# Fewer and wider score visits, a GLU in chunks of 256 tokens with gate and up in one bank, and attention output turned by DMA

## The chip, the cores and the metric

One core of a Trainium2 chip runs the whole program. The metric is the device time of one execution in microseconds. Three runs of the kernel before took 642.13 to 642.98 us, median 642.45.

## The reference

Two layers, each an attention part A and a gated part B, each with a residual, on x of 2048 tokens by 512 (bfloat16). Both layers use the same weights.

```python
def A(x, wqkv, wo):                      # 32 heads of 16, window of 256
    q, k, v = heads(x @ wqkv)
    s = q @ k.T * 16 ** -0.5
    s = where(0 <= i - j < 256, s, -1e9)
    return merge(softmax(s) @ v) @ wo
def B(x, w_gate, w_up, w_down):          # 512 -> 1792 -> 512
    return (sigmoid(x @ w_gate) * (x @ w_up)) @ w_down
for layer in range(2):
    x = x + A(layernorm(x), wqkv, wo)
    x = x + B(layernorm(x), w_gate, w_up, w_down)
```

## The kernel before, in words

Tokens stand in 16 tiles of 128. Scores are computed transposed: keys of tile t on the partitions, queries of tiles t, t+1 and t+2 (the window of 256) along the columns. A **visit** fills one PSUM tile, Sps (four banks, one buffer, line 335), by matmuls that use a quarter of the array's rows each (four heads side by side, `tile_position`), and one exp on ScalarE (line 339) writes the result to a ring in SBUF, PTring, of six slots per head. A visit before covers four heads and three query tiles, 1536 columns; at tiles 14 and 15 there are two or one query tile and 1024 or 512 columns. Eight visits make a key tile, 128 a layer, 256 in all. The ring's slots for the three query tiles are not always neighbours, so a visit takes one, two or three runs of four matmuls (`pieces`).

VectorE multiplies the diagonal block by a triangle (line 346), GpSimd clears the far corner of the third block (`affine_select`, line 351). When the three key tiles that a query tile needs are there, `values` (line 364) makes 48 small matmuls for half of the heads into OTps; VectorE copies that out as OTs (line 369). One visit later TensorE turns OTs by four transposes into PSUM (tps, line 381), VectorE divides by the row sums (Rt, line 389; On, line 391), SyncE issues a DMA transpose (OnT, line 395), and two visits later `oproj` (line 417) multiplies by wo; VectorE adds the residual (line 419) and begins the layer norm (lines 152 to 162), whose output a DMA transpose turns into xnT (line 174).

The projections take four tiles (512 tokens) at a time: q and k in chunks of 128 columns (line 237), v per tile (line 254), copied out by ScalarE. The GLU takes chunks of 128 of the 1792 columns: four gate matmuls (line 283) into one PSUM buffer, a tanh on ScalarE (line 286), four up matmuls (line 293) into another, and on VectorE hT = (tanh + 1) x up (line 295); w_down is halved once, so that this is the sigmoid. Then 14 down matmuls a tile (line 305). It does 512 tokens at a time, except that four of its ten streams take 256.

The order is made by a planner in `run`. It goes through the visits; in each it first issues the scores and the exp, then values where they are due, then what has been put off to this visit (`at`), and then pops units from the first stream that is ready (projections and GLU, in the order of a list) until the estimated TensorE time of the visit, T_SLOT, is used up. Each engine runs its instructions in that order. All of proj_ps, v_ps, gps, ups, dps, tps and OPps share three PSUM buffers (`ps_d`). The planner's figures only set the order; they are no times of the chip.

Of the kernel before, what the change touches and what calls it, by code (L numbers as in the profile page):

```python
# [8 lines left out]
ALU = mybir.AluOpType  # L9
# [33 lines left out]


class Stream:
# [5 lines left out]
    def add(self, ns, tag, fn):  # L51
        self.units.append((ns, tag, fn))

    def pop(self, done):
        ns, tag, fn = self.units.pop(0)
        fn()
        done.add(tag)
        return ns


class Net:
# [3 lines left out]
    def __init__(self, ctx, tc, A_x, wqkv, wo, w_gate, w_up, w_down, out):  # L65
# [17 lines left out]
        self.ontp = pool("on_t", 4)  # L83
# [14 lines left out]
        self.hT = big.tile([P, FC, TGW], BF16, name="hT")  # L98
# [32 lines left out]
        self.left = {}  # L131
        self.states = {}
# [68 lines left out]
    def proj_stream(self, kinds, L, tg):  # L201
        key = ("p", L, tg)
        gi = L * NTG + tg
        free = 0
        if "k" in kinds and gi >= 2:
            free = TGW // P * SLOTS_T * (gi - 1)
        if "v" in kinds and gi >= 3:
            free = max(free, (4 * (gi - 3) + 6) * SLOTS_T + 10)
        s = Stream(key, free)
        s.needs = [(key, t) for t in range(tg * NBG, (tg + 1) * NBG)]  # L210
        self.left[key] = self.left.get(key, 0)
# [19 lines left out]
    def _qk(self, key, tg, b, k, cq):  # L231
# [3 lines left out]
        c0 = (k == "k") * D + cq * P  # L235
        for kt in range(KT):
            nc.tensor.matmul(pt[:], lhsT=self.wq[:, kt, c0:c0 + P], rhs=xnT[:, kt, :],  # L237
                             start=(kt == 0), stop=(kt == KT - 1))
        self.used_up(key)
        if k == "q":  # L240
            nc.scalar.copy(out=self.qT[:, cq, tg * TGW:(tg + 1) * TGW], in_=pt[:])
            return
        kt = self.ktp.tile([P, TGW], BF16, name="kt")
        nc.scalar.copy(out=kt[:], in_=pt[:])
        for e in range(2):
            nc.vector.tensor_scalar(out=self.kTp[b][:, cq, e, :], in0=kt[:],
                                    scalar1=self.rms[e][:, 0:1], scalar2=None, op0=ALU.mult)

    def _v(self, key, tg, b, tt):
# [7 lines left out]
        nc.scalar.copy(out=vdst, in_=pt[:].rearrange("p (h e) -> p h e", e=16))  # L257
        self.used_up(key)

    def glu_stream(self, L, t0, n):  # L260
# [8 lines left out]
        for fc in range(FC):  # L269
            s.add(KT * (w / 2.4 + 3), None, lambda fc=fc: self._gate(key, fc, c0, w))  # L270
            s.add(KT * (w / 2.4 + 3), None, lambda fc=fc: self._up(key, fc, c0, w, last))
        cuts = [0, 5, 10, FC]
        for tt in range(n):
            for a, b in zip(cuts, cuts[1:]):
                s.add((b - a) * T_MM, ("d", L, t0 + tt, b), lambda tt=tt, a=a, b=b: self._down(L, t0 + tt, tt, a, b))
        return s

    def _gate(self, key, fc, c0, w):
# [6 lines left out]
        self.th = self.sigp.tile([P, TGW], BF16, name="gth")  # L285
        nc.scalar.activation(out=self.th[:, 0:w], in_=ps[:, 0:w], func=AF.Tanh, scale=0.5)  # L286

    def _up(self, key, fc, c0, w, last):
# [3 lines left out]
        for kt in range(KT):  # L292
            nc.tensor.matmul(ps[:, 0:w], lhsT=self.wu[:, kt, fc * P:(fc + 1) * P], rhs=xnT[:, kt, c0:c0 + w], start=(kt == 0),  # L293
                             stop=(kt == KT - 1))
        nc.vector.scalar_tensor_tensor(out=self.hT[:, fc, 0:w], in0=self.th[:, 0:w], scalar=1.0, in1=ps[:, 0:w],  # L295
                                       op0=ALU.add, op1=ALU.mult)
        if fc == FC - 1 and last:
            del self.xnT[key]

    def _down(self, L, t, tt, a, b):  # L300
# [6 lines left out]
        if b == FC:  # L307
            nc.vector.tensor_tensor(out=self.xsb[:, t, :], in0=self.xsb[:, t, :], in1=self.dps[:], op=ALU.add)
# [4 lines left out]

    def scores(self, L, t, g):
        nc = self.nc
        cq, e = g // 2, g % 2
        N = min(3 * P, S - t * P)
        nb = N // P  # L320
        order = sorted(range(nb), key=lambda b: ring_slot(t, b))
        p0 = ring_slot(t, order[0])
        step = ring_slot(t, order[1]) - p0 if nb > 1 else 1
        pieces = []
        for i, b in enumerate(order):
            if pieces and pieces[-1][1] + pieces[-1][2] == b:
                pieces[-1][2] += 1
            else:
                pieces.append([i, b, 1])
        kTp = self.kTp[(L * NTG + t // NBG) % 2]  # L330
        ko = (t % NBG) * P
        sps = self.sps
        for i, b, n in pieces:
            for m in range(4):
                nc.tensor.matmul(sps[:, m, i * P:(i + n) * P], lhsT=kTp[32 * m:32 * m + 32, cq, e, ko:ko + P],  # L335
                                 rhs=self.qT[32 * m:32 * m + 32, cq, (t + b) * P:(t + b + n) * P],
                                 start=True, stop=True, tile_position=(32 * m, 0))
# [239 lines left out]
```

## Time and profile before

| | |
|---|---|
| profiled execution | 641.7 us, its span 640.0 us |
| median of three runs | 642.45 us |
| first exp starts | 14.8 us |
| last exp starts | 583.8 us |
| busiest engines | TensorE 580.9 us, ScalarE 460.4 us, VectorE 423.5 us |
| exps | 256, 352.2 us of ScalarE |
| score matmuls | 1984 |
| transposes of OTs on TensorE | 256 matmuls, 25.6 us by modelled ends |

The span is the time from the first to the last instruction of the program on its engines. Rows of a timeline read: start, time taken, engine, line, operation, output and inputs, shape, count of merged instructions, and in brackets the engine's idle time ahead of it and what ended it. A group's row ends with its busy time, the mean time in ns of one, and the engine's idle time ahead of them. PE is TensorE, PEld its weight loads, ACT ScalarE, DVE VectorE, POOL GpSimd, SP SyncE.

### The profile page before, as it was taken

How to read it: one execution, taken by the hardware profiler on the slowest of the kernel's cores; microseconds unless marked ns; L12 is line 12 of the kernel's file. 1: busy time of each engine (PE TensorE's matmuls, PEld its weight loads, DVE VectorE, ACT ScalarE, POOL GpSimd, SP SyncE). 2: the span in 40 equal slices, each digit the busy share in tenths (PEclk: the TensorE clock that was granted, in tenths of full speed). 3: DMA queues.
4: the chain of work that ended last, by engine and by line, in shares of the span. 5: the costliest groups of instructions: out<-in, count | busy, mean ns of one | idle time of the engine just before them, and what ended most of it. 6: DMA issues, size and time to landing. Idle time of an engine off the chain costs nothing.

```text
span 640.0 us, 16976 instructions
## 1 busy us (share of the span) xinstructions
PE 580.9 (91%) x7216; PEld 281.8 (44%) x7216; DVE 423.5 (66%) x851; ACT 460.4 (72%) x497; POOL 166.4 (26%) x191
## 2 busy tenths in 40 slices
PE   4886789897779999899989999989999999999997
PEld 2333454553234444444434444444444444444675
DVE  5875577766556658865588666975766676665533
ACT  3998677787868897766877897679877886762221
POOL 3443223313323223310143222432222333100000
PEclk9998799999879999999999999999999999999999
DMA  7664400111100001100011000210011001101100
GB/s 229 106 169 116 127 18 19 23 26 27 18 13 18 17 18 24 34 18 17 19 34 34 16 17 18 43 27 14 11 27 42 18 18 34 31 18 27 38 18 16
DMA packets 63771, 24.95 MB, mean 39 GB/s; under 512 B 51664, under 2 KB 63696, under 8 KB 63696
## 3 DMA queue, kind: packets, MB, share of 16 engines
q1 hardware_dynamic: 63696, 23.87, 15.9%
q8 instruction: 56, 0.92, 0.6%
q14 instruction: 19, 0.16, 0.1%
HBM read 9.70 MB, written 2.10 MB: 18 GB/s over the span
## 4 chain that ended last, share of the span: by engine, by line
PE 58%; ACT 16%; DVE 14%; issue 6%; DMA 4%; POOL 1%; ACTq 0%; POOLq 0%; DVEq 0%
PE ups L293 13%; PE gps L283 13%; ACT PTring L339 13%; PE dps L305 9%; PE Sps L335 7%; PE OTps L364 5%; PE OPps L417 4%; DMA OnT<-On 3%; DVE ln_stats L152 3%; DVE xn L162 3%; DVE PTring L346 2%; PE proj_ps L237 2%; PE v_ps L254 2%; PE tps L381 2%; DVE OTs L369 1%
## 5 line engine op out<-in xcount | busy, mean ns | idle before, releaser
L339 ACT ACTIVATE PTring<-Sps 128x1536 bf16<-128x1536 f32 (+2 forms) x256 | 352.2, 1376 | 76.4 <-PE Sps L335 68.3
L351 POOL TENSOR_SCALAR_AFFINE_SELECT PTring<-PTring 128x1024 bf16<-128x1024 bf16 x112 | 127.3, 1138 | 168.3 <-ACT PTring L339 166.8
L295 DVE SCALAR_TENSOR_TENSOR hT<-gth,ups 128x512 bf16<-128x512 bf16 (+1 forms) x140 | 81.1, 579 | 74.7 <-PE ups L293 63.8
L283 PE MATMUL gps<-xnT,wg 128*128 128x512 bf16 (+1 forms) x560 | 122.7, 342 | 4.5 <-DMA xnT<-xn 2.1
L293 PE MATMUL ups<-xnT,wu 128*128 128x512 bf16 (+1 forms) x560 | 121.6, 340 | 3.4 <-DVE hT L295 2.3
L286 ACT ACTIVATE gth<-gps 128x512 bf16<-128x512 f32 (+1 forms) x140 | 71.5, 512 | 73.8 <-PE gps L283 71.4
L335 PE MATMUL Sps<-qT,kTp 32*128 32x128 bf16 (+2 forms) x1984 | 86.9, 246 | 27.5 <-ACT PTring L339 24.5
L305 PE MATMUL dps<-wd,hT 128*128 128x512 bf16 x448 | 108.3, 380 | 0.0
L155 POOL TENSOR_TENSOR ln_rs<-ln_rs,nhalf 128x1 f32<-128x1 f32 x64 | 38.3, 598 | 263.9 <-DVE ln_rs L154 259.1
L346 DVE TENSOR_TENSOR PTring<-PTring,maskq 128x1024 bf16<-128x1024 bf16 x128 | 97.2, 760 | 2.4 <-ACT PTring L339 2.4
L335 PEld LDWEIGHTS <-kTp 32*128 32x128 bf16 x1984 | 39.7, 92 | 129.1 <-issue 124.1
L283 PEld LDWEIGHTS <-wg 128*128 128x128 bf16 x560 | 51.4, 99 | 44.3 <-issue 7.6
L293 PEld LDWEIGHTS <-wu 128*128 128x128 bf16 x560 | 51.2, 98 | 41.9 <-issue 8.8
L237 PE MATMUL proj_ps<-xnT,wq 128*128 128x512 bf16 x256 | 63.7, 387 | 1.9 <-DMA xnT<-xn 1.1
L369 DVE CAST OTs<-OTps 128x512 bf16<-128x512 f32 x64 | 44.0, 687 | 26.0 <-PE OTps L364 25.3
L305 PEld LDWEIGHTS <-hT 128*128 128x128 bf16 x448 | 40.0, 98 | 44.2 <-issue 1.5
L364 PE MATMUL OTps<-PTring,Vaug 128*32 128x128 bf16 x2880 | 53.6, 224 | 0.0
L162 DVE TENSOR_SCALAR xn<-xsb,ln_mv,ln_rs 128x512 bf16<-128x512 bf16 x64 | 48.5, 761 | 7.3 <-POOL ln_rs L155 6.6
L419 DVE TENSOR_TENSOR xsb<-xsb,OPps 128x512 bf16<-128x512 bf16 x32 | 21.9, 686 | 46.9 <-PE OPps L417 46.9
L152 DVE BATCH_NORM_STATS2 ln_stats<-xsb 128x6 f32<-128x512 bf16 x64 | 44.3, 693 | 3.1 <-DMA xsb<-in_A_x_dram 1.4
L364 PEld LDWEIGHTS <-Vaug 128*32 128x32 bf16 x2880 | 42.2, 99 | 9.3 <-issue 5.5
L417 PE MATMUL OPps<-wot,OnT 128*128 128x512 bf16 x128 | 36.0, 397 | 3.7 <-DMA OnT<-On 3.6
(34 smaller groups left out, 295.6 us busy)
## 6 DMA issues: line engine op xcount, KB each, us to landing
out_dram<-xsb SPq DMA_DIRECT2D x16, 128.0 KB, 1.9
wg<-in_B_w_gate_dram SPq DMA_DIRECT2D x4, 448.0 KB, 4.1
wu<-in_B_w_up_dram SPq DMA_DIRECT2D x4, 448.0 KB, 4.1
wd<-in_B_w_down_dram SPq DMA_DIRECT2D x2, 896.0 KB, 5.4
wq<-in_A_wqkv_dram SPq DMA_DIRECT2D x3, 512.0 KB, 5.6
xsb<-in_A_x_dram SPq DMA_DIRECT2D x3, 512.0 KB, 8.5
OnT<-On SPq DMA_TRANSPOSE x64, 2.3
xnT<-xn SPq DMA_TRANSPOSE x60, 2.4
```

The source lines that it names most:

```text
L162: nc.vector.tensor_scalar(out=xn[:], in0=self.xsb[:, t, :], scalar1=mv[:, 0:1], scalar2=rs[:, 1:2], op0=ALU.subtract, op1=ALU.mult)
L237: nc.tensor.matmul(pt[:], lhsT=self.wq[:, kt, c0:c0 + P], rhs=xnT[:, kt, :], start=(kt == 0), stop=(kt == KT - 1))
L283: nc.tensor.matmul(ps[:, 0:w], lhsT=self.wg[:, kt, fc * P:(fc + 1) * P], rhs=xnT[:, kt, c0:c0 + w], start=(kt == 0), stop=(kt == KT - 1))
L286: nc.scalar.activation(out=self.th[:, 0:w], in_=ps[:, 0:w], func=AF.Tanh, scale=0.5)
L293: nc.tensor.matmul(ps[:, 0:w], lhsT=self.wu[:, kt, fc * P:(fc + 1) * P], rhs=xnT[:, kt, c0:c0 + w], start=(kt == 0), stop=(kt == KT - 1))
L295: nc.vector.scalar_tensor_tensor(out=self.hT[:, fc, 0:w], in0=self.th[:, 0:w], scalar=1.0, in1=ps[:, 0:w], op0=ALU.add, op1=ALU.mult)
L305: nc.tensor.matmul(self.dps[:], lhsT=self.hT[:, fc, tt * P:(tt + 1) * P], rhs=self.wd[:, fc, :], start=(fc == 0), stop=(fc == FC - 1))
L335: nc.tensor.matmul(sps[:, m, i * P:(i + n) * P], lhsT=kTp[32 * m:32 * m + 32, cq, e, ko:ko + P], rhs=self.qT[32 * m:32 * m + 32, cq, (t + ...
L339: nc.scalar.activation(out=self.ring[:, h0:h0 + 7:2, p0:p0 + (nb - 1) * step + 1:step, :], in_=sps[:, :, 0:N].rearrange("p w (b c) -> p w ...
L346: nc.vector.tensor_tensor(out=r0, in0=r0, in1=self.maskq[:].to_broadcast([P, 8, P]), op=ALU.mult)
L351: self.nc.gpsimd.affine_select(out=r2, in_=r2, compare_op=ALU.is_ge, fill=0.0, base=-1, pattern=[[0, 8], [-1, P]], channel_multiplier=1)
L364: nc.tensor.matmul(OT[32 * g:32 * g + 32, col, :], lhsT=Va[:, jj % NBG, VS * h:VS * h + 32], rhs=self.ring[:, h, ring_slot(jj, t - jj), :] ...
```

## The change

**Score visits.** Visits of kind A take eight heads and the two query tiles t and t+1; visits of kind B take sixteen heads and the query tile t+2 alone. Both are 2048 columns, at tile 15 kind A has 1024. A key tile takes four A and two B (at tiles 14 and 15 no B): 92 visits a layer, 184 in all. The fixed ring of slots is replaced by a table worked out at build time. The diagonal masks follow one visit after their A, the corner masks one and two visits after their B. `values` comes two visits after the end of its half (`PV_LATE`).

**GLU.** All of it goes in streams of 256 tokens. `_both` issues gate and up matmuls (256 wide) into the two halves of one PSUM bank, gups, then the tanh and the product. hT holds 256 tokens. There are 896 gate and 896 up matmuls, where there were 560 and 560 (336 of each were 512 wide), and 224 tanhs and products, where there were 140.

**Attention output.** `OT_DMA` is on: OTs is turned by a DMA transpose on SyncE's queue into Oq in SBUF, and VectorE's division reads Oq two visits later. The 256 transposes on TensorE are gone; 64 DMA transposes are new. OnT has three buffers, where it had four.

**Planner.** T_SLOT is 2500 in layer 0 and 2800 in layer 1 (it was 1900), the order list is new (q, v and k of layer 1 are streams of their own behind each four tiles of GLU), and the weight loads, the scaling of wd and layer 0's norms are put to lower visit numbers. Evictions are closures that are called by `flush`; with LAG off this is at once, as before. The count of all other instructions is the same.

```diff
-T_SC = 170
+T_SC = 240
-T_SLOT = 1900
+T_SLOTS = (2500, 2800)
+OT_LAG = 2
+LAG = False
+PV_LATE = (2, 2)
-OT_DMA = False
+OT_DMA = True
...
-        self.ontp = pool("on_t", 4)
+        self.ontp = pool("on_t", 3)
...
-        self.hT = big.tile([P, FC, TGW], BF16, name="hT")
+        self.hT = big.tile([P, FC, TGW // 2], BF16, name="hT")
...
+    def _both(self, key, fc, c0, w, last):
+        ps = self.ps_d.tile([P, 2, TGW // 2], F32, name="gups", tag="d")
+        for i, wt in enumerate((self.wg, self.wu)):
+            for kt in range(KT):
+                nc.tensor.matmul(ps[:, i, 0:w], lhsT=wt[:, kt, fc * P:(fc + 1) * P], rhs=xnT[:, kt, c0:c0 + w],
+                                 start=(kt == 0), stop=(kt == KT - 1))
...
+        def evac(eng):
+            th = self.sigp.tile([P, TGW], BF16, name="gth")
+            nc.scalar.activation(out=th[:, 0:w], in_=ps[:, 0, 0:w], func=AF.Tanh, scale=0.5)
+            nc.vector.scalar_tensor_tensor(out=self.hT[:, fc, 0:w], in0=th[:, 0:w], scalar=1.0, in1=ps[:, 1, 0:w],
+                                           op0=ALU.add, op1=ALU.mult)
...
+    def scores(self, L, t, kind, i):
+        slots = RING[L * NT + t]
+        nb = min(2, len(slots))
+        c0, n = (t * P, nb * P) if kind == "A" else ((t + 2) * P, P)
+        for cq in ((i,) if kind == "A" else (2 * i, 2 * i + 1)):
+            for e in range(2):
+                o = (e if kind == "A" else 2 * (cq % 2) + e) * n
+                for m in range(4):
+                    nc.tensor.matmul(self.sps[:, m, o:o + n], lhsT=kTp[32 * m:32 * m + 32, cq, e, ko:ko + P],
+                                     rhs=self.qT[32 * m:32 * m + 32, cq, c0:c0 + n],
+                                     start=True, stop=True, tile_position=(32 * m, 0))
+        if kind == "A":
...
+            nc.scalar.activation(out=out, in_=src, func=AF.Exp, scale=1.0 / float(np.sqrt(DH)))
+        else:
+            nc.scalar.activation(
+                out=self.ring[:, 16 * i:16 * i + 16, slots[2], :].rearrange("p (q m e) c -> p q m e c", q=2, e=2),
+                in_=self.sps[:].rearrange("p m (q e c) -> p q m e c", q=2, e=2),
+                func=AF.Exp, scale=1.0 / float(np.sqrt(DH)))
...
-            self.at(2, 0, lambda: self.norm(L, t, half, st, Oq))
+            self.at(OT_LAG, 0, lambda: self.norm(L, t, half, st, Oq))
...
-        order = [("kqv", 0, 0), ("kqv", 0, 1), ("qv", 0, 2), ("qv", 0, 3), ("g", 0, 0, 2), ("k", 0, 2), ("g", 0, 2, 2),
...
+        order = [("kqv", 0, 0, 4), ("kqv", 0, 4, 4), ("qv", 0, 8, 4), ("k", 0, 8, 4), ("qv", 0, 12, 4), ("k", 0, 12, 4)]
+        step = 2
+        for t in range(0, NT, step):
+            order.append(("g", 0, t, step))
+            if (t + step) % NBG == 0:
+                order += [(k, 1, t + step - NBG, NBG) for k in "qvk"]
+        order += [("g", 1, t, step) for t in range(0, NT, step)]
...
-            self.at((t - NBG) // 2 if t < 2 * NBG else t - 6, 0, lambda t=t: self.ln_later(("p", 0, t // NBG), t))
+            self.at((t - NBG) // 2 if t < 2 * NBG else (t - 6) * 3 // 4, 0, lambda t=t: self.ln_later(("p", 0, t // NBG), t))
...
-            self.at(3 + 2 * i, 0, fn)
-        self.at(26, 0, lambda: nc.vector.tensor_scalar(out=self.wd[:], in0=self.wd[:], scalar1=0.5, scalar2=None,
+            self.at(2 + 3 * i // 2, 0, fn)
+        self.at(19, 0, lambda: nc.vector.tensor_scalar(out=self.wd[:], in0=self.wd[:], scalar1=0.5, scalar2=None,
```

The order that comes out is shown at two places. The first is ScalarE in layer 0 at key tile 9 and the step to tile 10; in the kernel before PTring<-Sps is the exp of a visit and gth<-gps the tanh of a gate chunk of 512 tokens.

```order
L339 ACTIVATE PTring<-Sps 128x4x384
L286 ACTIVATE gth<-gps 128x512
L339 ACTIVATE PTring<-Sps 128x4x3x128
L286 ACTIVATE gth<-gps 128x512
L339 ACTIVATE PTring<-Sps 128x4x3x128 x2
```

The same engine, layer and key tiles in the changed kernel; 128x16x128 is an exp of kind B, 128x8x2x128 one of kind A, gth<-gups the tanh of a chunk of 256 tokens, and qT<-proj_ps a copy of a projection.

```order
L424 ACTIVATE PTring<-Sps 128x16x128
L422 ACTIVATE PTring<-Sps 128x8x2x128
L351 ACTIVATE gth<-gups 128x256 x2
L422 ACTIVATE PTring<-Sps 128x8x2x128
L351 ACTIVATE gth<-gups 128x256
L424 ACTIVATE PTring<-Sps 128x16x128
L276 CAST qT<-proj_ps 128x512
```

Where a tanh of 512 columns stood between two exps of 1536, one or two tanhs of 256 now stand between exps of 2048.

The second place is VectorE in layer 0 at about key tile 9, from the copy out of a half's values to its division. Before, OTs is the copy, Rt and On the division, hT the gated product:

```order
L369 CAST OTs<-OTps 128x512
L346 TENSOR_TENSOR PTring<-PTring,maskq 128x8x128
L389 RECIPROCAL Rt<-tps 128x16
L391 TENSOR_TENSOR On<-tps,Rt 128x256
L295 SCALAR_TENSOR_TENSOR hT<-gth,ups 128x512 x2
```

In the changed kernel, where xn is a normalised tile and the other ln rows its statistics:

```order
L455 CAST OTs<-OTps 128x512
L181 TENSOR_SCALAR xn<-xsb,ln_mv,ln_rs 128x512
L435 TENSOR_TENSOR PTring<-PTring,maskq 128x8x128 x2
L367 TENSOR_TENSOR xsb<-xsb,dps 128x512
L171 BN_STATS ln_stats<-xsb 128x6
L172 BN_AGGR ln_mv<-ln_stats 128x2
L173 TENSOR_SCALAR ln_rs<-ln_mv 128x1
L475 RECIPROCAL Rt<-Oq 128x16
L477 TENSOR_TENSOR On<-Oq,Rt 128x256
L181 TENSOR_SCALAR xn<-xsb,ln_mv,ln_rs 128x512
```

The division moved from one visit behind the copy to two, and its first instruction reads the tile that a DMA writes.

More of the change, by code (lines that the diff above doesn't have):

```diff
@@ L205, in proj_stream @@
         if "k" in kinds and gi >= 2:
[L206 removed]
+            free = self.first[divmod(4 * (gi - 1), NT)]
         if "v" in kinds and gi >= 3:
[L208 removed]
+            free = max(free, self.pv_slot[divmod(4 * (gi - 3) + 5, NT) + (1,)] + 1)
         s = Stream(key, free)
[L210 to L211 removed]
+        tiles = range(t0, t0 + n)
+        s.needs = [(key, t) for t in tiles]
+        self.left.setdefault(key, 3 * 4 * NBG)
         for cq in range(NCQ):
@@ L312, in _down @@
                 nc.sync.dma_start(out=self.out[0, t * P:(t + 1) * P, :], in_=self.xsb[:, t, :])
-    def scores(self, L, t, g):
-        nc = self.nc
[L318 to L329, printed above, removed]
+        return evac if b == FC else None
```

288 lines of the change are left out of this document (187 added, 101 removed), and 3 rows, old and new, of the table order.

## The prediction

> **What bounds the kernel now.** I read the page's first rows, then the stretches of 32 visits (a visit is one fill of the score tile and its exp; the stretches end where the 33rd, 65th ... exp starts), then the waits and the timeline.
>
> ```profile
> span 640.0 us, 16976 instructions
> PE 580.9 (91%) x7216; PEld 281.8 (44%) x7216; DVE 423.5 (66%) x851; ACT 460.4 (72%) x497; POOL 166.4 (26%) x191
> ```
>
> ```profile
> 14.80:91.90 77.10, 61.43 (x746) 30.96 (x745) 53.63 (x121) 63.64 (x74) 27.87 (x31) 0.91 0.46 110
> 91.90:163.10 71.20, 63.64 (x957) 35.29 (x955) 51.53 (x106) 56.85 (x62) 21.84 (x24) 1.00 0.12 23
> 163.10:236.80 73.70, 65.19 (x826) 28.70 (x825) 43.16 (x82) 59.00 (x59) 20.62 (x21) 0.91 0.08 16
> 236.80:306.30 69.50, 66.29 (x857) 30.08 (x856) 50.95 (x100) 48.90 (x57) 13.95 (x17) 1.00 0.12 25
> 306.30:376.80 70.50, 66.15 (x793) 29.09 (x792) 51.16 (x100) 57.53 (x57) 22.39 (x24) 1.00 0.12 24
> 376.80:448.20 71.40, 67.81 (x913) 30.77 (x912) 51.26 (x101) 57.69 (x56) 23.12 (x25) 1.00 0.12 24
> 448.20:517.60 69.40, 67.73 (x861) 30.32 (x860) 47.05 (x89) 55.96 (x53) 19.80 (x21) 1.00 0.11 25
> 517.60:583.80 66.20, 63.68 (x838) 28.90 (x837) 43.20 (x79) 44.08 (x48) 11.01 (x13) 1.00 0.10 24
> 583.80:640.00 56.20, 52.76 (x404) 34.89 (x403) 23.89 (x50) 11.92 (x30) 0.55 (x1) 1.00 0.09 27
> ```
>
> Columns: length, then PE, PEld, DVE, ACT, POOL busy, granted clock, DMA share, GB/s. From 236.8 on PE is busy 94 to 98% of every stretch: PE bounds there. In the first three it is 80 to 89%, and the clock is 0.91 in two.
>
> ```profile
> PE Sps L335 <- ACT PTring L339: 24.5, 47, 2.0
> ```
>
> The rest of layer 0 is lost on the single score tile: PE may refill it only when the exp has read it, and ACT may start only when it is full.
>
> **What PE pays.** Matmul ends are modelled, so I take start to start.
>
> ```profile
> 402.43 2.12 PE L305 MATMUL dps<-wd,hT 128*128 128x512 bf16 x9
> ...
> 404.48 0.34 PE L335 MATMUL Sps<-qT,kTp 32*128 32x384 bf16 x4
> ...
> 404.75 0.60 PE L417 MATMUL OPps<-wot,OnT 128*128 128x512 bf16 x2
> ...
> 577.38 1.03 PE L293 MATMUL ups<-xnT,wu 128*128 128x512 bf16 x4
> 578.34 0.23 PE L335 MATMUL Sps<-qT,kTp 32*128 32x128 bf16 x4
> 578.51 0.60 PE L417 MATMUL OPps<-wot,OnT 128*128 128x512 bf16 x2
> ...
> 589.86 0.85 PE L364 MATMUL OTps<-PTring,Vaug 128*32 128x128 bf16 x48
> 590.64 1.25 PE L305 MATMUL dps<-wd,hT 128*128 128x512 bf16 x5
> 591.73 0.39 PE L381 MATMUL tps<-ident,OTs 128*128 128x128 bf16 x4
> 591.96 4.05 PE L305 MATMUL dps<-wd,hT 128*128 128x512 bf16 x18
> ...
> 612.02 6.21 PE L305 MATMUL dps<-wd,hT 128*128 128x512 bf16 x28
> 618.06 0.60 PE L283 MATMUL gps<-xnT,wg 128*128 128x256 bf16 x4
> 618.50 0.60 PE L293 MATMUL ups<-xnT,wu 128*128 128x256 bf16 x4
> ```
>
> A 512-wide matmul costs (618.06 - 612.02)/28 = 0.216 us, a 256-wide one 0.44/4 = 0.109, a set of 48 value matmuls 0.78, four transposes 0.23. A score visit: nine matmuls from 402.43 end at 404.37, the next non-score one starts at 404.75, so 384 columns per row strip cost 0.38; by the second trio (577.38 + 0.86 = 578.24 to 578.51) 128 columns cost 0.27. Hence about 0.21 per visit, whatever its size, and 0.00042 per column. A visit of the changed kernel (512 columns per strip) costs 0.43.
>
> On PE the change therefore removes 72 visits x 0.21 = 15.1 us (256 become 184, columns unchanged), and 64 x 0.23 = 14.7 us of transposes; cutting 336 + 336 matmuls in two adds 672 x (2 x 0.109 - 0.216) = 1.3 us. Counted by these prices, all PE work is 556 us before and 528 after.
>
> **What ACT and the score tile pay.**
>
> ```profile
> 95.10 0.66 ACT L286 ACTIVATE gth<-gps 128x256 bf16<-128x256 f32 x2
> ...
> 95.71 1.45 ACT L339 ACTIVATE PTring<-Sps 128x1536 bf16<-128x1536 f32 x1
> ...
> 97.21 0.35 PE L335 MATMUL Sps<-qT,kTp 32*128 32x128 bf16 x12 [0.28 <-ACT PTring L339]
> ...
> 97.61 1.45 ACT L339 ACTIVATE PTring<-Sps 128x1536 bf16<-128x1536 f32 x1 [0.45 <-PE Sps L335]
> ```
> ```profile
> 437.19 1.46 ACT L339 ACTIVATE PTring<-Sps 128x1536 bf16<-128x1536 f32 x1
> 438.53 1.16 ACT L241 CAST qT<-proj_ps 128x512 bf16<-128x512 f32 x2
> ...
> 440.93 0.59 ACT L241 CAST qT<-proj_ps 128x512 bf16<-128x512 f32 x1
> 441.40 0.62 ACT L257 CAST Vaug<-v_ps 128x512 bf16<-128x512 f32 x1
> ```
> ```profile
> L339 ACT ACTIVATE PTring<-Sps 128x1536 bf16<-128x1536 f32 x224 | 326.3, 1457 | 67.6 <-PE Sps L335 59.5 <-DVE ln_stats L152 3.0 <-issue 2.1
> L339 ACT ACTIVATE PTring<-Sps 128x1024 bf16<-128x1024 f32 x16 | 16.3, 1021 | 4.5 <-PE Sps L335 4.5
> ```
>
> 512 columns more cost 1457 - 1021 = 436 ns (0.43 us taken). Alone, an exp of 2048 is 1.45 + 0.43 = 1.88; with work queued behind it the 1536-wide one holds ACT 1.34 (437.19 to 438.53), so the new one 1.77. A 512-wide copy then holds it 0.47, a 256-wide tanh 0.28 to 0.30 (two from 95.10 to 95.71). The score tile's own period is 1.90 now (95.71 to 97.61: exp, 0.05, scores 0.35, 0.05); with 0.43 more exp and 128 columns (0.05) more of scores it is 2.38 to 2.40.
>
> So visits get fewer but longer. Visit by visit, from the new order, I take the largest of PE's work, ACT's work and 2.40. Layer 0, query tiles 4 to 7, 24 visits: PE 24 x 0.43 + 92 x 0.216 + 144 x 0.109 + 8 x 0.78 = 52.0; ACT 53.1; 24 x 2.40 = 57.6; the largest each time, 59.2. All eight stretches of four tiles so: layer 0 61.1, 59.2, 59.0, 48.3 (the score tile decides in most visits, ACT where two projections are copied: 1.77 + 2 x 0.47 = 2.71); layer 1 67.4, 69.2, 70.1, 54.4 (PE decides: for tiles 4 to 7 24 x 0.43 + 124 x 0.216 + 232 x 0.109 + 8 x 0.78 = 68.5). From the last exp on: 400 x 0.109 + 120 x 0.216 + 2 x 0.78 + 0.43 = 71.5 of PE without a wait, as 583.8 to 640 shows now. Sum 560.2; with the 14.8 ahead of the first exp, which the change leaves alone, and 3.5 behind the last matmul (56.2 less the 52.7 counted for the last stretch) 578.5.
>
> The same count for before, with 1.96 as period, gives 67.6, 66.6, 67.2, 67.4, 68.1, 68.7, 68.7, 65.0 for its stretches; the trace has 9.5, 4.6, 6.5, 2.1, 2.4, 2.7, 0.7, 1.2 more. I carry this excess over except the third stretch's 6.5: there PE starved in six visits with 0.4 to 1.2 us of work, which the new order fills. That is 23.2: span 601.7. The profiled run's time was 641.7 at a span of 640.0, so 603.4, and its median lies 0.75 above that: 603.
>
> What I cost at nothing: hT at half size and one buffer (a chunk's first down matmuls come after its last gate, and read the first chunks); weight loads, the scaling of wd and layer 0's normalisations at lower visit numbers (visits are longer by about the same factor, so they fall at much the same times; SP's queue takes them in the same order); three OnT buffers for four (a pair is read two visits after it is issued, the next pair comes six visits later); masks, which still end a visit ahead of their values. DVE pays 224 tanh products at 0.42 for 81.1 us now, so 13 us more in all:
>
> ```profile
> L295 DVE SCALAR_TENSOR_TENSOR hT<-gth,ups 128x256 bf16<-128x256 bf16 x56 | 23.5, 420 | 25.5 <-PE ups L293 19.9 <-ACT gth L286 5.0 <-ACT PTring L339 0.3
> xnT<-xn SPq DMA_TRANSPOSE x60, 2.4
> ```
>
> DVE has room (43 to 52 us now in stretches of 66 to 74, and 1 to 2 us more in each) except in the first stretch, where the 53.6 us now in 77.1 must go into 61 to 70. The turned output adds 64 transposes on SP's queue and a wait of DVE for each: behind it stand a normalised tile, masks and adds. Two visits (4.8 us) less scores, values and copy out (0.43 + 0.78 + 0.69) leave 2.9 us for a transfer that takes 2.4: bounds 0 and, one transfer queued ahead, about 1.2 to 1.9 late. I take 0, nearest the 2.4.
>
> **Clock.**
>
> ```profile
> 54.40:57.80 3.40, 1.43 (x14) 0.41 (x12) 0.00 (x0) 3.07 (x4) 0.26 (x1) 1.00 0.91 226
> 57.80:68.00 10.20, 6.86 (x112) 3.57 (x108) 4.57 (x10) 7.25 (x5) 2.52 (x3) 0.50 0.51 163
> ```
> ```profile
> 57.52 0.34 PE L335 MATMUL Sps<-qT,kTp 32*128 32x384 bf16 x4 [1.97 <-ACT PTring L339]
> ```
>
> 3.4 us with PE busy 1.43 were followed by 10.2 us at half clock, with no idle gap over 1.97. In the new order visits 18 and 19 hold 1.29 and 1.21 us of work in 2.40, so one such dip stays likely; it is in the first stretch's 9.5. The Trainium skill (TensorE: Matmul & The Clock Gate, Why this matters for your kernels) asks only that no PE-idle gap exceeds about 3 us; no visit here has one, so by that rule there is no dip and the sum is some 8 us lower, 595. The trace, which dips after a gap of 1.97 us, disagrees.
>
> **Rivals.** (1) The forecast, 0.60: 597 to 610. (2) Less excess, 0.13: no dip and a first stretch that flows, 8 to 14 us less, 589 to 595. For it: its visits are fuller; against: three engines have over 50 us to do there. (3) The turned output comes late in layer 0, 0.14: 32 halves x 0.3 to 0.9 us = 10 to 29 us, 613 to 632. For it: the 0.5 us margin; against: PE's slack of 0.2 to 0.3 in a visit. (4) More half clock, 0.07: layer 0 falls to half clock again and again, as in the two stretches of 0.91 now (2 x 0.09 x 77.1 + 2 x 0.09 x 73.7 = 27 us of it, half of that lost): 9 to 15 us more, 612 to 618. (5) Slower or no gain, 0.06: that DVE wait falls into both layers and holds masks, hence values, hence the next scores, each time; it decides from 39/64 = 0.61 us per half on, and at 0.8 us gives 654. Against it: layer 1's visits of 2.9 us give 1 us more margin. That the change doesn't do what it says is in (5) too: were the exp's cost purely by the column, 1.457 x 2048/1536 = 1.94 for 1.88 and layer 0's visits 0.06 longer, 92 x 0.06 = 5.5 us, inside the range.
>
> **Numbers.** Range 588 to 625: it leaves out (5) and the far ends of (3). About 0.2% (1.3 us) is what a measurement of this kernel can tell from no change. Faster 0.94, same 0.01, slower 0.05.
>
> **What would show it.** Right: 184 exps of about 1.88, start to start 2.4 in layer 0 and 2.9 in layer 1, score visits of 0.43 on PE, no L381 group, last exp at about 527. Wrong: exps 2.6 or more apart in layer 0, DVE idle ahead of Rt until a DMA, half clock over more than 10 us, or ACT waiting in the last stretch.

## The result and the profile after

The changed kernel takes 610.91 us (median of 4 runs, 608.51 to 615.70), the kernel before 642.29 beside it: a ratio of 0.9522 [0.9456, 0.9588]. The forecast was 603, the range 588 to 625. The profiled execution took 608.51.

The page's first rows, answering to the two of before:

```profile
span 606.8 us, 17707 instructions
PE 549.5 (91%) x7568; PEld 332.9 (55%) x7568; DVE 433.4 (71%) x935; ACT 457.0 (75%) x509; POOL 175.7 (29%) x191
```

TensorE is busy for 31 us less, for the same share of the span. The stretches, with the columns of the prediction's table: four key tiles each (24 visits, in the fourth and eighth row 20), the first four rows layer 0, the next four layer 1, and from the last exp to the end:

```profile
14.96:87.45 72.49, 54.51 (x677) 26.18 (x676) 48.10 (x111) 60.83 (x60) 24.32 (x28) 0.93 0.53 128
87.45:149.34 61.89, 54.45 (x877) 31.83 (x876) 46.47 (x95) 55.33 (x55) 22.39 (x22) 1.00 0.18 36
149.34:212.19 62.85, 54.48 (x877) 31.76 (x876) 47.86 (x99) 55.24 (x56) 22.34 (x22) 1.00 0.22 44
212.19:260.63 48.44, 45.40 (x733) 26.00 (x734) 41.94 (x92) 39.78 (x40) 16.61 (x17) 1.00 0.26 40
260.63:332.69 72.06, 68.06 (x937) 40.30 (x930) 58.08 (x125) 59.17 (x65) 21.14 (x22) 1.00 0.25 46
332.69:402.34 69.65, 69.31 (x997) 42.30 (x996) 53.48 (x118) 59.41 (x65) 24.35 (x24) 1.00 0.26 42
402.34:477.17 74.83, 70.67 (x1009) 43.66 (x1008) 52.80 (x110) 60.10 (x68) 23.02 (x22) 1.00 0.20 39
477.17:532.06 54.89, 54.80 (x830) 36.27 (x829) 41.17 (x87) 42.24 (x50) 14.87 (x14) 1.00 0.20 40
532.06:606.80 74.74, 71.34 (x616) 51.82 (x614) 35.63 (x81) 20.07 (x52) 1.10 (x2) 1.00 0.12 29
```

Layer 0 takes 245.7 us, where it took 291.5 (77.10 + 71.20 + 73.70 + 69.50); the rest takes 346.2 for 333.7. Part of layer 0's gain is thus work handed on: behind the last exp PE has 71.34 us to do, for 52.76. In layer 1 PE is busy 94 to 100% of each stretch. In layer 0 it is not, and the waits say why (us in total, times, longest):

```profile
ACT PTring L422 <- PE Sps L408: 30.6, 43, 2.1
PE Sps L408 <- ACT PTring L422: 17.5, 36, 1.2
DVE Rt L475 <- DMA Oq<-OTs: 9.5, 7, 2.2
PE OPps L503 <- DMA OnT<-On: 8.9, 8, 4.4
PE gups L344 <- DVE hT L352: 3.5, 5, 1.0
```

The exchange between score tile and exp still leads (PE waits 17.5 us for the exp, where it was 24.5). New is the wait for Oq: the turned output is late seven times. The wait of PE for OnT, ahead of the output projection, was 3.6 us before with 1.5 at most (`PE OPps L417 <- DMA OnT<-On`); it is 8.9 now, with one of 4.4.

### The profile page after: what moved, and what is told of

It reads as the page before. It is cut to its first block, busy times and chain, and to the rows that moved or that the text cites. A ratio compares the mean times of both kernels' runs of the same rounds, so it can differ in the third digit from the quotient of the medians.

```text
span 606.8 us, 17707 instructions
## 1 busy us (share of the span) xinstructions
PE 549.5 (91%) x7568; PEld 332.9 (55%) x7568; DVE 433.4 (71%) x935; ACT 457.0 (75%) x509; POOL 175.7 (29%) x191
## 4 chain that ended last, share of the span: by engine, by line
PE 55%; ACT 16%; DVE 13%; DMA 7%; issue 6%; POOL 2%; SPq 0%; ACTq 0%; DVEq 0%; POOLq 0%
PE gups L344 24%; PE dps L362 13%; ACT PTring L422 10%; PE Sps L408 6%; DMA OnT<-On 5%; PE OTps L450 4%; PE OPps L503 4%; PE proj_ps L258 3%; DVE ln_stats L171 3%; ACT PTring L424 2%; DVE PTring L435 2%; DMA xnT<-xn 2%; DVE xn L181 2%; PE v_ps L285 1%; DVE kTp L269 1%
## 5 line engine op out<-in xcount | busy, mean ns | idle before, releaser
L422 ACT ACTIVATE PTring<-Sps 128x2048 bf16<-128x2048 f32 (+1 forms) x128 | 234.7, 1834 | 31.0 <-PE Sps L408 30.6
L437 POOL TENSOR_SCALAR_AFFINE_SELECT PTring<-PTring 128x1024 bf16<-128x1024 bf16 x112 | 133.4, 1212 | 74.4 <-ACT PTring L424 74.4
L351 ACT ACTIVATE gth<-gups 128x256 bf16<-128x256 f32 x224 | 82.2, 386 | 77.1 <-PE gups L344 64.8
L344 PE MATMUL gups<-xnT,wg 128*128 128x256 bf16 x896 | 136.1, 275 | 4.2 <-DVE hT L352 3.5
L344 PE MATMUL gups<-xnT,wu 128*128 128x256 bf16 x896 | 135.1, 274 | 0.0
L352 DVE SCALAR_TENSOR_TENSOR hT<-gth,gups 128x256 bf16<-128x256 bf16 x224 | 90.3, 416 | 57.2 <-ACT gth L351 56.8
L424 ACT ACTIVATE PTring<-Sps 128x2048 bf16<-128x2048 f32 x56 | 105.4, 1882 | 11.2 <-PE Sps L408 10.5
L344 PEld LDWEIGHTS <-wg 128*128 128x128 bf16 x896 | 82.0, 98 | 30.3 <-issue 11.5
L408 PE MATMUL Sps<-qT,kTp 32*128 32x128 bf16 (+1 forms) x1920 | 73.4, 246 | 27.7 <-ACT PTring L422 17.5
L435 DVE TENSOR_TENSOR PTring<-PTring,maskq 128x1024 bf16<-128x1024 bf16 x128 | 95.8, 752 | 0.3 <-ACT PTring L422 0.2
L344 PEld LDWEIGHTS <-wu 128*128 128x128 bf16 x896 | 88.0, 98 | 10.5
L258 PE MATMUL proj_ps<-xnT,wq 128*128 128x512 bf16 x256 | 63.8, 388 | 3.4 <-DVE hT L352 1.8
L450 PE MATMUL OTps<-PTring,Vaug 128*32 128x128 bf16 x2880 | 52.7, 221 | 1.2 <-DVE PTring L435 1.1
L450 PEld LDWEIGHTS <-Vaug 128*32 128x32 bf16 x2880 | 41.1, 97 | 14.6 <-issue 10.5
L503 PE MATMUL OPps<-wot,OnT 128*128 128x512 bf16 x128 | 35.5, 386 | 10.2 <-DMA OnT<-On 8.9
```

Of the source, the lines that this page charges most:

```text
L258: nc.tensor.matmul(pt[:, 0:w], lhsT=self.wq[:, kt, c0:c0 + P], rhs=xnT[:, kt, o:o + w], start=(kt == 0), stop=(kt == KT - 1))
L344: nc.tensor.matmul(ps[:, i, 0:w], lhsT=wt[:, kt, fc * P:(fc + 1) * P], rhs=xnT[:, kt, c0:c0 + w], start=(kt == 0), stop=(kt == KT - 1))
L351: nc.scalar.activation(out=th[:, 0:w], in_=ps[:, 0, 0:w], func=AF.Tanh, scale=0.5)
L408: nc.tensor.matmul(self.sps[:, m, o:o + n], lhsT=kTp[32 * m:32 * m + 32, cq, e, ko:ko + P], rhs=self.qT[32 * m:32 * m + 32, cq, c0:c0 + n] ...
L422: nc.scalar.activation(out=out, in_=src, func=AF.Exp, scale=1.0 / float(np.sqrt(DH)))
L424: nc.scalar.activation(out=self.ring[:, 16 * i:16 * i + 16, slots[2], :].rearrange("p (q m e) c -> p q m e c", q=2, e=2), in_=self.sps[:]. ...
```

## The experiments

### The visits alone, and the turn put back on TensorE

`visits_alone` keeps the new visits and planner, but takes the GLU 512 tokens at a time, gate and up in a buffer each, and turns on TensorE. `turn_on_pe` only turns on TensorE.

```diff
# both
-OT_DMA = True
+OT_DMA = False
# visits_alone
-        self.hT = big.tile([P, FC, TGW // 2], BF16, name="hT")
+        self.hT = big.tile([P, FC, TGW], BF16, name="hT")
-        step = 2
+        step = 4
```

> Of the change only the score visits and the planner's figures: the GLU in chunks of 512 tokens with gate and up in two banks, the output turned by TensorE. Forecast's theory: 72 visits x 0.21 = 15.1 us of TensorE work less than before, but layer 0 bound by the period of 2.40 with less GLU work ready early; the sum of the largest per visit is 587.3 against 594.9 for the kernel before and 573.5 with the GLU by 256 tokens: 632 to 638 us. Rival, the visits carry the whole gain: 611 to 618 us. Rival, wide visits lose by themselves: above 642 us.

> The changed kernel with the attention output turned by TensorE again (four transposes a half, no transfer), all else as changed. Forecast's theory: 64 x 0.23 = 14.7 us of TensorE work come back; in layer 0 the score tile's period of 2.40 us hides about half a visit's share, so the sum of the largest of TensorE, ScalarE and 2.40 per visit grows from 563.1 to 573.5: 10 us slower than the changed kernel's 611, about 621 us. Rival, the turned output comes late: the new wait on the transfer costs VectorE and what is queued behind it as much as the transposes did, so it is no slower than 611 us.

`visits_alone` takes 638.87, ratio 0.9946 [0.9928, 0.9964], just over what was expected; `turn_on_pe` 612.35, ratio 0.9526 [0.9504, 0.9549], near the rival's end. So the visits alone bring about 3.5 us, the GLU's new form 26.5 on top of them, and the turn by DMA 1.4 more, within the spread of these runs. (`visits_alone` has all of the GLU at 512 tokens; before, four of the ten streams took 256.) In its profile, the longest of its ten executions (642.18), layer 0 takes 248.1 us and the rest 377.8, for 291.5 and 333.7 before: what the visits save in layer 0 comes back later. In the way of the prediction's sum (visit by visit the largest of PE, ACT and 2.40; the numbers are in the expectations) the visits were to bring 7.6 us (594.9 to 587.3), the GLU's form 13.8 (to 573.5) and the turn by DMA 10.4 (to 563.1), of that 2.3 to 2.5 in layer 0. The first stretch of `turn_on_pe` and its last:

```profile
14.96:83.96 69.00, 54.41 (x712) 26.77 (x711) 48.67 (x116) 61.12 (x61) 24.62 (x29) 0.98 0.53 122
...
517.67:609.80 92.13, 88.71 (x752) 64.53 (x749) 41.54 (x94) 24.80 (x64) 1.10 (x2) 1.00 0.08 21
```

The last is 17.4 us longer than with the turn by DMA (92.13 for 74.74), since the transposes fill the visits and GLU work is left over. But the first is 3.5 shorter, at a granted clock of 0.98 for 0.93. In these profiles layer 0 takes 243.1 (245.7 with the DMA), the rest 351.7 (346.2).

### The GLU's new form without the new visits, and one bank made two

`glu256_alone` is the kernel before with all GLU streams at 256 tokens, gate and up in a buffer each. `glu256_turn` has the half-size hT and the turn by DMA too. `two_banks` is the changed kernel with gate and up as two units in a buffer each, as before.

```diff
# glu256_alone and glu256_turn, so for each stream of four tiles
-("g", 0, 4, 4)
+("g", 0, 4, 2), ("g", 0, 6, 2)
# glu256_turn
-OT_DMA = False
+OT_DMA = True
# two_banks
-            if n <= 2:
+            if n <= 1:
```

> The kernel before with every GLU stream at 256 tokens (gate and up still in two banks), nothing else. Forecast's theory: 672 x 0.0025 = 1.7 us more TensorE work, and visits filled less evenly by the smaller units; the sum of the largest of TensorE, ScalarE and 1.96 per visit grows from 594.9 to 602.7: about 650 us, slower than before. Rival, smaller chunks start the GLU earlier and shorten the whole: below 640 us.

> The kernel before with every GLU stream at 256 tokens, hT at half size, and the output turned by a DMA transpose two visits ahead of its division. Forecast's theory: 14.7 us of TensorE work less, but mostly in visits that the score tile's period of 1.96 bounds: the sum falls by 3.1 from the 602.7 with the GLU alone to 599.6, so 3 us faster than that kernel, about 647 us. With visits of 2.1 us, two of them leave 2.3 us for a transfer of 2.4 to 2.5: rival, it comes late each time and VectorE's wait shows, 5 us or more slower than with the GLU alone.

> The changed kernel with gate and up of a 256-token chunk again in two PSUM buffers, as two units of the planner (0.44 us of TensorE each, so visits are filled more closely: 2.41 us of TensorE work per visit of layer 0 from key tile 4 on, for 2.17). Theory, TensorE work against the period is all that counts: the sum of the largest per visit falls from 563.1 to 553.6, so 9 us less, about 601 us. Rival, the three shared PSUM buffers: each chunk now holds two of them until the tanh behind an exp of 1.88 us and the product are done, TensorE waits for hT, and it is as slow as 611 us or slower, the more the chunks in a visit; then the single bank is what made 256 tokens pay here and not in the kernel before (660 us).

`glu256_alone`: 660.34, ratio 1.0273 [1.0242, 1.0304], slower as expected and by 10 us more. In its list of PE's waits the buffers of up show, for 2.3 us in the kernel before (`PE ups L293 <- DVE hT L295`):

```profile
PE ups L293 <- DVE hT L295: 6.6, 12, 0.9
PE ups L293 <- DVE On L391: 5.4, 11, 0.7
```

`glu256_turn`: 654.74, 1.0182 [1.0156, 1.0208], so there the turn by DMA, with hT at half size, brings 5.6. `two_banks`: 651.65, 1.0162 [1.0137, 1.0187], 41 us behind the changed kernel; my theory (TensorE's work against the period is all that counts, 601) falls. Waits of PE in `two_banks`:

```profile
PE gps L317 <- DVE hT L335: 17.5, 17, 2.7
...
PE ups L331 <- ACT gth L322: 10.7, 18, 0.9
...
PE ups L331 <- DVE hT L335: 6.9, 12, 1.9
```

These three are 35.1 us, where the changed kernel's one row of the kind (`PE gups L344 <- DVE hT L352`) has 3.5. By the count of the three shared buffers, a chunk that takes two of them lets PE be at most one and a half chunks ahead of the tanh and the product, a chunk in one bank three. The granted clock is lower too: 0.973 to 0.976 in its five executions, that is 16 to 18 us less of it in 650 ((1 - 0.975) x 650), for 5 to 10 in the changed kernel's four. What this run can't part is the bank and the units' order: with two buffers gate and up are separate units of the planner too.

### The exp at half its size

The exps from layer 0's key tile 6 on run over half the columns; the softmax lacks the other half of the scores there. It shows what the score tile's period is worth.

```diff
-            if nb == 2:
+            if nb == 2 and (L or t >= 6):
+                src = self.sps[:].rearrange("p m (e b c) -> p (m e) b c", e=2, c=P)[:, :, 0, :]
+                out = self.ring[:, 8 * i:8 * i + 8, slots[0], :]
+            elif nb == 2:
...
+            q = 1 if L or t >= 6 else 2
```

> The changed kernel with every exp from key tile 6 of layer 0 on over half of its columns (1024 of 2048; the other half of the scores is computed but not read, and the ring keeps old values there), so that the score tile's period falls from 2.40 to about 1.55 us. Forecast's theory, the period bounds layer 0 and TensorE bounds layer 1: layer 0's stretches of key tiles 4 to 7, 8 to 11 and 12 to 15 fall from 61.9, 62.8 and 48.4 us to 56 to 58, 52 to 55 and 44 to 46; layer 1's three full stretches by 1 to 4 us each; in all 585 to 595 us. Rival, layer 0 is bound by VectorE or by transfers: its stretches fall by under 3 us each, 605 us or more.

596.94, ratio 0.9306 [0.9284, 0.9329], just over the theory's 585 to 595 and well under the rival's 605. The third and fourth stretch:

```profile
145.97:205.54 59.57, 53.73 (x870) 30.46 (x876) 49.01 (x99) 36.10 (x55) 23.05 (x22) 0.97 0.25 46
205.54:252.07 46.53, 43.86 (x726) 25.00 (x734) 42.40 (x92) 27.13 (x39) 17.06 (x17) 1.00 0.22 42
```

ACT loses 13 to 19 us there (55.24 to 36.10, 39.78 to 27.13), the stretches only 3.3 and 1.9; with the second (58.1 for 61.9) that is 9.0 us, where the theory had 14 to 21. Layer 1's hardly move (69.9, 69.8, 73.8, 54.3). So the score tile does hold up layer 0's last three stretches, but for 9 us of 173 only: in the two shown PE's waits for the exp fall from 6.8 to 0.3 us, PE is then busy 90 and 94% of the time, and its waits for OnT there rise from 1.3 to 4.8. In the whole program, for 8.9 in the changed kernel:

```profile
PE OPps L507 <- DMA OnT<-On: 11.3, 9, 4.8
```

### When the turned output is read, and the projection behind it

`turn_lag1` reads Oq one visit after the transpose is issued, `oproj_lag3` multiplies by wo one visit later.

```diff
# turn_lag1
-OT_LAG = 2
+OT_LAG = 1
# oproj_lag3
-ON_LAG = 2
+ON_LAG = 3
-        self.ontp = pool("on_t", 3)
+        self.ontp = pool("on_t", 4)
```

> The changed kernel with the division one visit behind the copy of the values instead of two. The transfer of about 2.5 us then has some 0.5 us in layer 0 and 1 us in layer 1 before VectorE reaches the division. Forecast's theory, the two visits hide the transfer: VectorE now waits 1.5 to 2 us in each of 64 halves ahead of Rt (100 us or more in total, 9.5 us in the changed kernel), with masks and products queued behind it; a third of it reaches the end, 630 to 645 us. Rival, nothing important stands behind the division: within 3 us of 611 us.

> The changed kernel with the output projection three visits behind its transfer instead of two, and four OnT buffers for three. TensorE's waits on OnT (8.9 us ahead of the matmuls, 14.9 us ahead of their weight loads) should go. Theory: they are a part of the first stretch's excess (up to 4.6 us at once), so 3 to 8 us less, 603 to 608 us, mostly in layer 0. Rival, the score tile's period hides them: within 2 us of 611 us.

`turn_lag1`: 640.03, ratio 0.9982 [0.9956, 1.0009], within what was expected. Its wait for Oq:

```profile
DVE Rt L475 <- DMA Oq<-OTs: 43.0, 35, 3.0
```

33.5 us more of this wait cost 29.1 us, and mostly in layer 1, whose first three stretches grow to 79.1, 78.7 and 81.5. The time agrees with the expectation partly by luck: I had 100 us or more of waits with a third of them reaching the end, and it was 43.0 in 35 halves of 64, with nearly all of the increase reaching it. A late division does cost what rival (5) feared, and the second visit of delay keeps it away. The way is another one: PE's waits for the masks (`PE OTps L450 <- DVE PTring L435`) are 3.6 us for 1.1, but those for VectorE's products, which free the shared buffers (`PE gups L344 <- DVE hT L352`), are 15.0 for 3.5. `oproj_lag3`: 611.71, ratio 0.9534 [0.9508, 0.9560]; PE's wait for OnT falls from 8.9 to 1.5 us, and nothing is gained. With the projection a visit later the residual and the norm are later too: `PE proj_ps L258 <- DMA xnT<-xn` is 5.1 us there, for 0.8. The rival's number was right; its reason, the score tile's period, isn't shown, since half clock takes more here too (9.9 us of PE's time on average over four executions, 7.8 in the changed kernel's).

### More work in a visit of layer 0

```diff
-T_SLOTS = (2500, 2800)
+T_SLOTS = (2650, 2800)
```

> The changed kernel with the planner's time for a visit of layer 0 at 2650 for 2500, so that one more unit goes into most visits from key tile 4 on (TensorE work per visit 2.7 us instead of 2.17) and less is left behind the last exp (40 us of TensorE instead of 71). Theory: where TensorE work exceeds the period of 2.40, nobody waits; the sum of the largest per visit falls from 563.1 to 558.7, 4 us faster, about 607 us. Rival, the excess grows with a third eviction in a visit: 611 us or slower.

614.72, ratio 0.9582 [0.9558, 0.9605]: no gain. The tail shrinks to 52.16 us, but layer 0 takes 275.6, and PE comes up against data that isn't there yet:

```profile
PE gups L344 <- DMA xnT<-xn: 11.5, 6, 3.5
```

The clock falls as well, and takes more than these waits. Its granted share is 0.955 to 0.963 in the four executions, which is 23 to 28 us of PE's time, for 5 to 10 in the changed kernel's. In the profile most of it lies in the first stretch:

```profile
15.19:92.69 77.50, 60.53 (x701) 31.29 (x709) 51.54 (x117) 62.72 (x65) 24.02 (x28) 0.82 0.51 120
```

### The turn by DMA in a part of the kernel

Layer 1 alone, layer 0 alone, and all but layer 0's first four key tiles; elsewhere TensorE turns.

```diff
-        if OT_DMA:
+        if L == 1:                # turn_l1_dma
+        if L == 0:                # turn_l0_dma
+        if L == 1 or t >= 4:      # turn_l0_late_dma
```

> The changed kernel with the turn on TensorE in layer 0 and by DMA in layer 1. The sum of the largest per visit is 565.6 (563.1 as changed, 573.5 all on TensorE). Theory, the transfer's waits ate the gain: 7.5 us more excess with the DMA than without, of which 4 in layer 0's first stretch beside the weight loads; those go, so 604 to 609 us, best of the three. Rival, the waits belong to layer 1 (72.1 and 74.8 us against sums of 67.4 and 70.1): they stay and 2.5 us come on top, 612 to 615 us.

> The changed kernel with the turn by DMA in layer 0 and on TensorE in layer 1; the sum is 571.2. Theory: layer 0 keeps its waits and layer 1 gets 7.4 us of TensorE work back, 614 to 619 us, the worst of the three. Rival, layer 1's transfer cost more than it saved: 605 to 611 us.

> The changed kernel with the turn on TensorE in layer 0's key tiles 0 to 3 and by DMA everywhere else. Theory: what the turn by DMA costs in layer 0 sits in its first stretch (72.5 and 74.8 us with it, 69.0 and 69.6 without, and 10.2 us of half clock in place of 3.4), while the last stretch of the layer gains by it (48.4 and 48.1 for 51.2). Then the first stretch is about 69.5 with at most one dip of 3.4 us, the next three 62, 63 and 48.5, and the time is 601 to 605. Rival: the transfers cost all along layer 0 (or through what else is on SyncE's queue), so that it comes out between the kernel with the turn by DMA in layer 1 alone (603.8) and the changed kernel (610.9), 606 to 611, with the first stretch still at 72 or more.

`turn_l1_dma`: 603.83, ratio 0.9412 [0.9385, 0.9438]; `turn_l0_dma`: 618.83, 0.9651 [0.9626, 0.9677]; `turn_l0_late_dma`: 605.69, 0.9455 [0.9437, 0.9472]. Against `turn_on_pe` (612.35) the DMA wins 8.5 us when it turns layer 1 and loses 6.5 when it turns layer 0; by the ratios to the kernel before that ran beside each, it is 7 and 8. The first stretches of the three, in this order:

```profile
15.47:85.11 69.64, 55.47 (x713) 27.08 (x712) 49.10 (x115) 61.34 (x62) 24.49 (x28) 0.98 0.56 120
```
```profile
14.73:89.57 74.84, 53.91 (x677) 25.58 (x677) 47.69 (x111) 60.87 (x60) 24.90 (x28) 0.93 0.52 124
```
```profile
14.96:83.92 68.96, 53.56 (x706) 27.00 (x711) 48.59 (x116) 61.12 (x62) 24.62 (x29) 0.98 0.52 122
```

Without the DMA's transposes in the first four key tiles the stretch is 69 us at 0.98, with them 72.5 to 75 at 0.93: the place is as the theory said. The other half of the theory fails: the layer's last stretch is 50.87 in `turn_l0_late_dma`, not 48.5, so the turn by DMA wins nothing there. The total is between theory and rival: 605.69 is 5.2 below the changed kernel, and not below `turn_l1_dma`. That one is the best version found.

All executions together say more of the clock. (1 - granted clock) x span, what the throttle took of PE's time, is 4.9, 8.6, 7.3 and 10.4 us in the changed kernel's four (clock 0.992, 0.986, 0.988, 0.983), 4.9 to 8.7 in `turn_l0_dma` (mean 5.9), and only 0.0 to 2.4 in `turn_on_pe` (mean 1.5) and 0.0 to 4.2 in `turn_l1_dma`. So of the 6.5 us that layer 0 loses to the turn by DMA, up to 4.4 (5.9 less 1.5) are clock. In `visits_alone` it is 10.2 to 18.6 (mean 12.7), so up to 11 of the 26.5 us that the GLU's form brings are clock too, which the prediction's sum doesn't have.

## Why the prediction was right, and where its size was off

The sum held in total; the median is 7.9 us above the point and 0.9 above the 597 to 610 that I gave to the forecast itself. Its shares did not hold. By the same count visits, GLU and turn were to bring 7.6, 13.8 and 10.4 us, 31.8 together, and they brought about 3.5, 26.5 and 1.4, 31.4 together (in this order of adding). The GLU gave 12.7 more and the other two 13.1 less, and that these cancel is luck. Of my signs of being wrong three came: exps 2.6 or more apart in layer 0 (2.67 on average, 245.7/92), VectorE idle ahead of Rt until a DMA, and half clock over more than 10 us (10.2). The first stood against my own sum, which gives 2.65 for layer 0 ((61.1 + 59.2 + 59.0 + 48.3 + 16.2)/92). Step by step:

**Visits on PE: right.** Four 512-wide down matmuls from 117.09 end at 117.95, and the next non-score matmul starts at 118.38, so a visit costs 0.43, as forecast.

```profile
117.09 1.03 PE L362 MATMUL dps<-wd,hT 128*128 128x512 bf16 x4
118.05 0.40 PE L408 MATMUL Sps<-qT,kTp 32*128 32x256 bf16 x8
118.38 0.61 PE L344 MATMUL gups<-xnT,wg 128*128 128x256 bf16 x4
```

**Exps and period: right for the undisturbed visit.** 1.88 us by the groups below (176 exps; the other 8, of half the width, take 1.02). With work queued behind it an exp holds ACT 346.91 - 345.14 = 1.77. Exps with nothing between them on ACT, held up by the scores alone, start 2.38 and 2.44 apart (110.38, 112.76, 115.20).

```profile
L422 ACT ACTIVATE PTring<-Sps 128x2048 bf16<-128x2048 f32 x120 | 226.5, 1888 | 26.0 <-PE Sps L408 25.8
...
L424 ACT ACTIVATE PTring<-Sps 128x2048 bf16<-128x2048 f32 x56 | 105.4, 1882 | 11.2 <-PE Sps L408 10.5
```
```profile
110.38 1.88 ACT L422 ACTIVATE PTring<-Sps 128x2048 bf16<-128x2048 f32 x1 [0.66 <-PE Sps L408]
112.76 1.88 ACT L422 ACTIVATE PTring<-Sps 128x2048 bf16<-128x2048 f32 x1 [0.50 <-PE Sps L408]
115.20 1.88 ACT L424 ACTIVATE PTring<-Sps 128x2048 bf16<-128x2048 f32 x1 [0.56 <-PE Sps L408]
```
```profile
345.14 1.88 ACT L422 ACTIVATE PTring<-Sps 128x2048 bf16<-128x2048 f32 x1
346.91 0.59 ACT L276 CAST qT<-proj_ps 128x512 bf16<-128x512 f32 x1
```

On average layer 0's exps start 2.55 apart from its fifth key tile on ((61.89 + 62.85 + 48.44)/68) and 3.02 in the first stretch (72.49/24), not 2.4; layer 1's 2.98 ((532.06 - 260.63)/91) for 2.9.

**The sum by stretches: 5.1 us short, by misses that partly cancel.** The stretches exceed their sums by 11.4, 2.7, 3.8, 0.1 in layer 0, 4.7, 0.5, 4.7, 0.5 in layer 1 and -0.3 at the end; I carried over 9.5, 4.6, 0, 2.1, 2.4, 2.7, 0.7, 1.2. What exceeds it is the first stretch (1.9), the third (3.8) and two of layer 1 (2.3 and 4.0), 12.0 together; the other five fall short by 7.1. In the third I had dropped all of the 6.5 us of before, and 3.8 came back. The rest of the miss is that the profiled execution was the shortest of the four, 2.4 us to the median where I had allowed 0.75, and a slip: 601.7 + 1.7 + 0.75 is 604.2, not 603.

**The turned output at no cost: the step that failed.** I bounded its lateness by 0 and 1.2 to 1.9 us and took 0. It was late seven times, 9.5 us in all and up to 2.2. In six of the seven the transfer itself took 2.41 to 2.46 us, as counted; what failed was the 2.9 us of room, since it was issued up to 3.3 us after the copy or VectorE came sooner. One thing I did not look at cost PE more at once: the On that it delays has to go through the same queue once more, as OnT, and the weight loads that the change moves to lower visit numbers stand in that queue. SP's queue and PE in the first stretch:

```profile
46.88 0.57 SPq L598 DMA_DIRECT2D wu<-in_B_w_up_dram  x1
47.50 0.50 SPq L598 DMA_DIRECT2D wg<-in_B_w_gate_dram  x1
48.10 1.17 SPq L481 DMA_TRANSPOSE OnT<-On  x1
```
```profile
52.46 1.03 PE L503 MATMUL OPps<-wot,OnT 128*128 128x512 bf16 x2 [4.39 <-DMA OnT<-On]
```

The same place in the chain of waits (start, time, what), and in stretches:

```profile
48.10 4.31 DMA OnT<-On
```
```profile
48.40:51.80 3.40, 0.00 (x0) 0.00 (x0) 0.00 (x0) 1.08 (x1) 0.00 (x0) 1.00 1.03 297
...
51.80:55.20 3.40, 2.74 (x10) 0.81 (x14) 1.57 (x3) 0.00 (x0) 0.00 (x0) 0.54 1.03 291
```

The transpose was issued at 48.10, behind two loads of 448 KB each, and took 4.31 us; the median OnT lands after 2.3. For 4.39 us PE did nothing while the DMA engines were busy throughout, and then the clock fell to half. In `turn_on_pe` On is ready a visit earlier, only one of the two loads is ahead, and PE waits 0.3 us for OnT in the whole program. I costed weight loads at nothing because SP's queue "takes them in the same order"; the order between them and the transposes is what changed.

That the loads make the 4.31 is not shown. No run moved the loads alone, and 12 other OnT of the changed kernel, issued after 100 us when no load was left, took 3.4 to 4.4 us as well, such as this one:

```profile
326.14 4.44 DMA OnT<-On
```

Nor is it shown that this wait makes the first stretch long. `oproj_lag3` brings PE's waits for OnT down to 1.5 us, and its first stretch is no shorter, at a granted clock of 0.91 (13.7 us at half clock, for 10.2):

```profile
15.21:87.69 72.48, 53.54 (x659) 25.45 (x665) 49.81 (x107) 60.62 (x60) 25.62 (x27) 0.91 0.58 128
```

What the runs show is the place and the size: without the DMA's turn in the first four key tiles the stretch is 3.5 us shorter, with 3.4 us at half clock. By which wait the turn lengthens it stays open. So rivals (3) and (4), late output and more half clock in layer 0, each came true in small. Most of the DVE wait of rival (5) stays away at a lag of two.

**The GLU: right for a reason that I had not given.** I charged its matmuls 1.3 us and let the pieces of 256 and the single bank do nothing else. On PE that is so (the 13.8 us of its share in the sum come from GLU work that is ready earlier). But my sum lets PE go on whenever it has work, and with two buffers per chunk, in two units, that is not true for pieces this short. `glu256_alone` is 17.5 us slower than the kernel before, where the sum had 7.8 (594.9 to 602.7); `two_banks` is 41 us behind the changed kernel, where the sum had it 9.5 ahead. So the kernel's gain hangs on a line of the change that I took for a detail.

**Clock: one dip expected, three came**, 10.2 us in all (from 28.20, 52.09 and 75.99), all in the first stretch. For a single dip the prediction took off 8 us; 10.2 us at half clock are 5.1 of PE's time. The first dip is not the turn's, whose first transpose is issued at 32.10. What stood ahead of the third:

```profile
72.20:76.00 3.80, 1.59 (x72) 1.21 (x72) 3.28 (x5) 3.23 (x4) 2.60 (x3) 1.00 0.57 162
```
```profile
73.10 0.40 PE L408 MATMUL Sps<-qT,kTp 32*128 32x256 bf16 x8 [1.05 <-ACT PTring L422]
73.43 0.85 PE L450 MATMUL OTps<-PTring,Vaug 128*32 128x128 bf16 x48
75.53 0.41 PE L408 MATMUL Sps<-qT,kTp 32*128 32x128 bf16 x16 [1.24 <-ACT PTring L422]
```

PE was busy 1.59 of 3.80 us, with no gap over 1.24. The Trainium skill (TensorE: Matmul & The Clock Gate, Why this matters for your kernels) asks for gaps under about 3 us; the dip behind the gap of 4.39 agrees with it, this one does not. The traces point to the busy share instead. Every spell of half clock, but for one at a trace's end, lasts a multiple of 3.41 us; so each of the 14 traces can be cut into windows of 3.41 us with all changes of the clock at their borders. Of the full-clock windows with PE busy (by its modelled ends) for under 42%, all 32 were followed by half clock; at 42 to 50% 18 of 27, at 50 to 60% 2 of 39, above that none of 2298.

## What to carry to other kernels

A transfer that replaces work on a busy engine is free only where the queue that issues it is; count what else that queue is given, and follow the result to the next transfer on it. Before a loop is cut into smaller pieces, count the buffers that a piece holds until its last reader is done: here gate and up as one unit in one PSUM bank, against two units in two, decides between 4.8% faster and 1.6% slower. When an engine is relieved in a stretch where it already waits, its clock may fall; take such a change only where the engine is the bound, as `turn_l1_dma` does.

## What the hardware showed besides

The division's product was 0.42 us when it read PSUM, and reads two SBUF tiles now. Its groups, of before and of after:

```profile
L391 DVE TENSOR_TENSOR On<-tps,Rt 128x256 bf16<-128x256 bf16 x64 | 27.2, 424 | 2.2
```
```profile
L477 DVE TENSOR_TENSOR On<-Oq,Rt 128x256 bf16<-128x256 bf16 x64 | 36.1, 564 | 2.2
```

One that meets GpSimd's `affine_select`, and one that doesn't:

```profile
104.15 2.51 POOL L437 TENSOR_SCALAR_AFFINE_SELECT PTring<-PTring 128x1024 bf16<-128x1024 bf16 x2
...
104.69 1.03 DVE L477 TENSOR_TENSOR On<-Oq,Rt 128x256 bf16<-128x256 bf16 x1
```
```profile
135.31 0.43 DVE L477 TENSOR_TENSOR On<-Oq,Rt 128x256 bf16<-128x256 bf16 x1
```

Of the 64, the 30 with no select beside them take 425 ns on average, the 34 others 686, and up to 1207 (15 of them 424 to 428 all the same). The Trainium skill (SBUF — State Buffer, SBUF: two separate sides) has a VectorE operation with two SBUF inputs and a GpSimd operation that reads SBUF exclude each other; the trace agrees. It is 8.9 us of VectorE's time that the prediction did not count, on the way from Oq to OnT.
